# A fourth block product at half size in layer two's gate/up passes, and a step list for each of the four passes

## Chip, cores and metric

The kernel runs on one core of a Trainium2 chip. The time is the device time of one execution in microseconds, median of several runs; the lower is the better. The engines are TensorE (PE: matrix products; PEld is its weight load), VectorE (DVE), ScalarE (ACT), GpSimd (POOL) and SyncE (SP), which issues every DMA of this kernel. Each runs its own queue in order and waits for others at semaphores. Matrix products land in eight banks of PSUM, which VectorE and ScalarE read and write; everything else lies in SBUF.

## The reference

Two blocks are applied twice each, A, B, A, B, with the same weights, to x of 2048 tokens by 1024:

```python
phi = lambda t: jnp.where(t > 0, t + 1, jnp.exp(t)) + 1e-6
# block A (linear attention, 32 heads of 32)
q, k, v = split(layernorm(x) @ wqkv)
kv = einsum("bhsd,bhse->bhde", phi(k), v); z = sum over s of phi(k)
x = x + ((phi(q) @ kv) / (phi(q) . z + 1e-6)) @ wo
# block B (gated, no activation)
h = (layernorm(x) @ w_gate) * (layernorm(x) @ w_up)     # 1024 -> 3584
x = x + h @ w_down                                       # 3584 -> 1024
```

## The kernel before

**Layers and passes.** Block A and block B together are called a layer here; layer one is the first A and B (`first=True`), layer two the second. `layer_B` works on two passes of 1024 tokens (`ps_` 0 and 1). Each pass is a gate/up stage (`gateup`) that fills h, and a down stage (`down`) that adds h @ w_down to x. So there are four gate/up passes in all.

**Block products.** A gate/up pass runs over 14 pairs `p` of units. A unit is 256 columns of w_gate (even p) or of w_up (odd p); the two units of a pair, A and B, go through the same steps beside each other. One unit is a 2 x 2 block product (weights in blocks of 512 x 128, tokens in blocks of 512 x 512), made in Winograd's form of Strassen's scheme with seven products in place of eight, numbered 1 to 7. A whole product is four matmuls of 512 columns, accumulated in one bank (line L1534). The sums of weight blocks that products 3, 5, 6, 7 need are made once, in the first pass of layer one (`prep_s`), stored to `s_scratch` and loaded afterwards.

**Half-size products.** The same product number of both units, A and B together, is again a 2 x 2 block product, over blocks half as large. If its number is in the set that `L2SETS` names for the pass, it is made from seven half-size steps of two matmuls of 256 columns each (L1652) instead of two whole products. Steps 1, 5, 6, 7 work in two small banks (`B_L2`, 5 and 6, which swap roles from product to product); steps 2, 3, 4 (`direct`) add into the product's own bank. Around them stand copies and sums, `l2_of`: step 1 is followed by a ScalarE copy that seeds half of the first destination bank (L1656), step 5 by a ScalarE copy to SBUF named c5 (L1668), step 6 by a VectorE sum that seeds the other half (`seed5`, L1659) and reads step 6's bank, step 7 by both a copy and a sum for the second bank. The set before is "5" for the first pass of layer one, "542" for the second, and "254" for both passes of layer two. Product 1 can be in the set too, for pairs from 2 on (`p > 1`); no pass of the kernel before has it there.

**Further sums.** Half-size products need sums of weight blocks (`sums24`, `sums5`) and of token blocks (`tp_ops`). Those of weights are made in layer one, stored (`p4scr`, `p5scr`, `p1scr`, all called p_scratch in the profile) and loaded for each pair later (`load_s24`, `load_s5`, `load_s1`). `sp1buf` says where those for product 1 lie.

**The order of the work.** For each pair `gateup` runs through a list of tokens in `ORDERS`, chosen by the pass's set of products. The engines' queues follow it:

- `P1A` is product 1 of unit A, `D3B` product 3 of unit B into its final bank, or steps 2 and 3 (A) or 4 (B) where product 3 is made at half size; `41` is step 1 of half-size product 4.
- `F1A` evicts block 1 of unit A to h (`mul`, L917 on VectorE; for odd p GpSimd multiplies at L1558; a few evictions go through ScalarE). `S24`, `S5`, `S1` make or load the sums.
- `R` lets `ring_issue` load the next two units into a ring of five slots. `T0`, `T1` call `ticks`: layer norm steps of other tokens (`micro`), in the first pass of layer one also sums of weights (L914). `HA`, `HB` act in the last pair only.
- An apostrophe means that the token acts for the pair before, and a plus for the pair after. Tokens with an apostrophe that are left at the end form the `tail`, which is issued behind the first seven matmuls of the down stage (L1973).

Matmuls of half-size down products have line L2054. L914 is the helper for plain sums on VectorE, L917 that for a scaled sum, and L589 is that for a DMA.

**The planner.** `P.reorder` may rearrange, by a cost model, the instructions that carry one of the tags it is given; the others keep the order of the program. Before, the gate/up stage of layer one's second pass (`gu1`) is among the tags; the other three gate/up passes are not.

**Layer norm ahead of time.** While layer one's second gate/up pass runs, `ticks1` takes the first eight tokens' blocks of the next block A through layer norm in small steps (three a block, `micro`) up to `LN_G1`.

Of the kernel before, what the change touches and what calls it, by code (L numbers as in the profile page):

```python
# [334 lines left out]
def build_kernel(nc, A_x, A_wqkv, A_wo, B_w_gate, B_w_up, B_w_down, out):  # L335
# [16 lines left out]
    START_LATE = False  # L352
    TQ_N = 3
    LN_G1 = 8

    L2SETS = {(False, 0): "5", (False, 1): "542", (True, 0): "254", (True, 1): "254"}
    ORDERS = {
# [5 lines left out]
    }  # L363
    MUL_ENG = "pool"
    DORDS = {(True, 0): "4125637", (True, 1): "2167453", (False, 0): "2167453", (False, 1): "2167453"}
# [124 lines left out]
    with ExitStack() as es:  # L490
# [168 lines left out]
        class LN:  # L659
# [15 lines left out]
            def dst(self, n):  # L675
                if self.to == "A0":
                    return xr[:, n, :], r_xr(n)
                if self.to == "B" and n < 8 and n % 4 > 1:
                    o = RE + 2048 * (n % 4)
                    return vh(o, D), R(o, D * 2)  # L680
                return xn[n % 2], R(O_XN[n % 2], D * 2)

# [325 lines left out]
            dma(v, p5scr[p].rearrange("p (i x) -> p i x", i=4), [x for y in r for x in y], KL5[p % 2 if ps_ and not first else 0], rd=R(V_SP + p * 96 + 32, 32))  # L1008

        def sp1buf(first, ps_, m):  # L1010
            if not first and ps_:
                return (xnT[:, 4:8, 256 * m:256 * m + 256], [R(O_XT + (4 + i) * S * 2 + 512 * m, 512) for i in range(4)])
            o = RE + 4096 if first else O_X + (1 - m) * D * 2
            return vh(o, 1024).rearrange("p (i x) -> p i x", i=4), [R(o + i * 512, 512) for i in range(4)]
# [69 lines left out]
        def layer_A(lnp, nxt, first):  # L1084
# [369 lines left out]
            for i in range(NST):  # L1454
                if na[0] < NST:
                    if i % 3 == 2:
                        norm(tok[na[0]])
                        na[0] += 1
                elif RG["n"] < NR and i >= RING_I:
                    ring_issue()  # L1460
                nxt.step_t(1)
                nxt.b1_one()
                if i >= 2 and not START_LATE:
                    nxt.start(i - 2)
                y_grp(tok[i], 0, i)
                y_seed(i + 1)
                if i >= 1 and START_LATE:
                    nxt.start(i - 1)
                if i < NST - 1:
                    nxt.b2_one()  # L1470
                y_grp(tok[i], 1, i)
                if i > 3 and tws:
                    tws.pop(0)()
                if i in (11, 12, 13, 14):
                    stash(i - 7)
                if i == 14 and not first:
                    load_s24(0, 0)
                    load_s24(0, 1)
                    load_s5(first, 0, 0)
                if RG["tq"] is None:  # L1480
                    RG["tq"], RG["tn"] = [], 0
                while RG["tn"] < 4 and nxt.t_next > 4 + RG["tn"]:
                    RG["tq"] += t_ops(0, RG["tn"])
                    RG["tn"] += 1
                    if RG["tn"] == 4:
                        RG["tq"] += tp_ops(0, L2SETS[not first, 0].replace("1", ""))
                for _ in range(TQ_N):
                    if RG["tq"]:
                        RG["tq"].pop(0)()
# [5 lines left out]
        def layer_B(lnp, nxt, first):  # L1495
# [11 lines left out]
            def pair(ps_, p, l2):  # L1507
# [99 lines left out]
                    return v.rearrange("p i (k c) -> p i k c", k=2), r  # L1607

                def sums5(q="5"):
                    if not first or ps_:  # L1610
                        if q == "1":
                            load_s1(ps_, p)
                        else:
                            load_s5(first, ps_, p)
                        return
                    sp, rp = sp3() if q == "5" else sp1()
                    wA, rA = units[0]["w"][q]
                    wB, rB = units[1]["w"][q]
                    tt(sp[:, 0], wB[:, 0:2, :], wB[:, 2:4, :], ALU.add, rB, rp[0])
                    tt(sp[:, 2], wA[:, 0:2, :], wB[:, 0:2, :], ALU.subtract, rA + rB, rp[2])  # L1620
                    tt(sp[:, 1], sp[:, 0], wA[:, 0:2, :], ALU.subtract, rA + rp[0], rp[1])
                    tt(sp[:, 3], wA[:, 2:4, :], sp[:, 1], ALU.subtract, rA + rp[1], rp[3])
                    if q == "1":
                        dma(p1scr[p].rearrange("p (i x) -> p i x", i=4), sp1buf(first, ps_, m)[0], R(V_SP + p * 96 + 64, 32), KP1, rd=[x for y in rp for x in y])
                        return
                    dma(p5scr[p].rearrange("p (i x) -> p i x", i=4), sp5buf(first, ps_, m)[0], R(V_SP + p * 96 + 32, 32), KP5[m], rd=[x for y in rp for x in y])
# [87 lines left out]
            def gateup(ps_, ticks, l2, hook):  # L1714
                jit = first and ps_ == 0
                NP = NU // 2
                pairs = [pair(ps_, p, l2) for p in range(NP)]
                order = ORDERS[l2].split()
                n0 = RG["at"]["g", ps_]

                def token(p, tk, tail_):
# [18 lines left out]
                        return  # L1740
                    if tk[0] == "T":
                        i = int(tk[1])
                        if jit:
                            if i:
                                store_s(n0 + 2 * p)
# [9 lines left out]
                    c = pairs[p]  # L1755
                    if tk == "S1" and not first and p < 2:
                        return
                    if not first and (tk == "S24" and p < 2 or tk == "S5" and p < 1 + ps_) or first and ps_ and tk[0] == "S" and p == 0:
                        return
                    if tk == "S24":  # L1760
                        c["sums24"]()
# [11 lines left out]
                if jit:  # L1773
                    prep_s(n0)
                    prep_s(n0 + 1)
                for tk in ("S24", "S5"):
                    if tk + "+" in order:
                        token(-1, tk + "+", False)
                for p in range(NP):
# [406 lines left out]
            def dticks1(q, t):  # L2186
                if is_last:
                    return
                o1 = DORDS[first, 1]
                if q == o1[1] and t == 3:  # L2190
                    for x in "567":
                        tw_back("k", x)
# [12 lines left out]
                wd_load(1)  # L2205
            tq, pend = [], []
            pre, go = down(0, dticks0)
            tail = gateup(0, ticks0, L2SETS[not first, 0], pre)
            lnp.need(NST - 1)
            tq += t_ops(1) + tp_ops(1, "254" if first else L2SETS[not first, 1].replace("1", "")[::-1])  # L2210
            go(tail)
            pre, go = down(1, dticks1)
            P.tag = "gu1" if first else None
            tail = gateup(1, ticks1, L2SETS[not first, 1], pre)
            P.tag = None
            go(tail)
            lnp.use_dma = False
            lnp.on_act = False
# [32 lines left out]
        layer_A(lnA, lnB, False)  # L2251
        layer_B(lnB, None, False)

        P.reorder({"kq2", "gu1", "g1", "y1"})
        P.plan()
        P.emit(nc, block, esem, dsem, [KOUT])
    return P
# [34 lines left out]
```

## Time and profile before

| what | value |
|---|---|
| median of 3 runs | 1443.44 us (1442.42 to 1444.73) |
| the profiled execution | 1443.52 us, of which its span on the engines 1441.8 us |
| granted TensorE clock | 1.000 of full speed |
| GpSimd busy, share of the span | 439.5 us, 30% |
| moved by DMA | 337.80 MB, mean 234 GB/s |
| HBM read / written | 248.38 MB / 66.85 MB |

The profile is that of one execution. Busy times are given by engine, by group of instructions (line of the kernel, engine, operation, out<-in shapes, count; then busy time, mean of one in ns, and the idle time ahead of them with what ended it) and by stretch of time. The chain of waits follows the work back from the last instruction, at each step to what released it. In a timeline each row is a start in us, a duration, the engine, line and operation, the number of instructions merged, and in square brackets the idle time ahead with what ended it. TensorE's matmuls are pipelined: one is listed with a duration longer than its distance to the next.

### The profile page before, as it was taken

Reading aid. Unit: us, or ns where it says so; the run is one execution under the profiler, and the core shown is the slowest. Engines: PE = TensorE matmul, PEld = TensorE weight load, DVE = VectorE, ACT = ScalarE, POOL = GpSimd, SP = SyncE. Lnnn points to the kernel's source line nnn. Section 1 sums busy time; section 2 is a strip of 40 time slices with the busy share of each in tenths; the row PEclk is TensorE's granted clock in tenths of the full one; section 3 lists DMA queues with packets and bytes.
Section 4 is the critical chain, followed back from the end, with each engine's and each line's share of the span. In section 5 each row is a group of like instructions: output and inputs, shape, how many; then the busy total and the mean of one; then the engine's idle time right before and its main releaser. Section 6 shows DMA issues by size and latency. Waiting matters only on the chain.

```text
span 1441.8 us, 22143 instructions
## 1 busy us (share of the span) xinstructions
PE 1430.4 (99%) x8273; PEld 795.9 (55%) x8273; DVE 1156.2 (80%) x2170; ACT 597.4 (41%) x1220; POOL 439.5 (30%) x436
## 2 busy tenths in 40 slices
PE   9999999999999999999999999999999999999999
PEld 4444444555544555566664444456666576666558
DVE  8988898988868797887899869876666896666597
ACT  4332365454400255551147723555555014555302
POOL 4543631211110053432014446215343102342400
PEclk9999999999999999999999999999999999999999
DMA  7446766999999998986783656678886779888667
GB/s 241 101 108 178 159 156 172 279 325 308 288 311 324 304 297 259 291 275 209 279 269 95 190 162 142 177 184 260 272 254 227 254 247 297 265 272 274 228 203 236
DMA packets 350428, 337.80 MB, mean 234 GB/s; under 512 B 106736, under 2 KB 294640, under 8 KB 350320
## 3 DMA queue, kind: packets, MB, share of 16 engines
q1 hardware_dynamic: 350320, 336.38, 77.0%
q8 instruction: 65, 1.06, 0.3%
q14 instruction: 43, 0.35, 0.1%
HBM read 248.38 MB, written 66.85 MB: 219 GB/s over the span
## 4 chain that ended last, share of the span: by engine, by line
PE 90%; DVE 5%; DMA 2%; ACT 2%; issue 1%; SPq 0%; DVEq 0%; ACTq 0%
PE ps L1534 28%; PE ps L1652 14%; PE ps L1973 13%; PE ps L1094 8%; PE ps L1437 8%; PE ps L2054 8%; PE ps L1329 7%; PE ps L1158 3%; DVE arena L917 2%; DVE arena L914 1%; DMA arena<-in_A_wqkv_dram 1%; DMA arena<-p_scratch 1%; DMA arena<-xn_scratch 1%; PE ps L1352 0%; DVE ps L1659 0%
## 5 line engine op out<-in xcount | busy, mean ns | idle before, releaser
L1534 PE MATMUL ps<-arena 128*128 128x512 f16 x2016 | 491.3, 379 | 0.0
L917 DVE SCALAR_TENSOR_TENSOR arena<-ps,arena 128x512 f16<-128x512 f32 (+2 forms) x562 | 366.4, 681 | 62.4 <-PE ps L1973 27.6
L1558 POOL TENSOR_TENSOR arena<-arena 128x512 f16<-128x512 f16 x196 | 225.2, 1170 | 489.2 <-DVE arena L917 488.7
L914 DVE TENSOR_TENSOR arena<-arena 128x512 f16<-128x512 bf16 (+7 forms) x584 | 311.7, 575 | 11.3 <-PE ps L2054 4.9
L1534 PEld LDWEIGHTS ps<-arena 128*128 128x128 bf16 (+1 forms) x2016 | 196.8, 98 | 166.1 <-DVE arena L917 0.7
L1652 PE MATMUL ps<-arena 128*128 128x256 f16 x1960 | 273.4, 273 | 3.4 <-DVE ps L1659 1.6
L1652 PEld LDWEIGHTS ps<-arena 128*128 128x128 f16 (+1 forms) x1960 | 188.2, 98 | 106.5 <-DVE ps L1659 15.7
L1539 ACT ACTIVATE arena<-ps 128x512 f32<-128x512 f32 x308 | 184.4, 599 | 146.6 <-PE ps L1534 146.2
L1659 DVE TENSOR_TENSOR ps<-ps,arena 128x256 f32<-128x256 f32 x280 | 120.2, 429 | 142.7 <-ACT ps L1656 66.0
L1973 PE MATMUL ps<-arena 128*128 128x512 f16 (+1 forms) x896 | 195.2, 379 | 0.0
L1656 ACT COPY ps<-ps 128x256 f32<-128x256 f32 x280 | 98.5, 363 | 177.2 <-PE ps L1652 120.9
L1973 PEld LDWEIGHTS ps<-arena 128*128 128x128 f16 x896 | 87.4, 98 | 104.7
L2054 PE MATMUL ps<-arena 128*128 128x256 f16 (+1 forms) x1176 | 129.8, 273 | 0.2
L1094 PE MATMUL ps<-arena 128*128 128x512 bf16 x576 | 127.1, 379 | 0.5 <-DMA arena<-in_A_wqkv_dram 0.5
L2054 PEld LDWEIGHTS ps<-arena 128*128 128x128 f16 x1176 | 114.7, 98 | 15.6 <-ACT ps L2060 1.0
L1329 PE MATMUL ps<-arena 128*128 128x512 bf16 x512 | 115.8, 379 | 1.2 <-DMA arena<-xn_scratch 0.8
L1437 PE MATMUL ps<-arena 128*128 128x512 bf16 x512 | 110.8, 379 | 0.0
L1223 POOL TENSOR_TENSOR arena<-arena 128x1024 f16<-128x1024 f32 x32 | 80.0, 2498 | 86.6 <-DVE arena L1221 81.9
L1117 POOL TENSOR_TENSOR arena<-arena 128x512 f32<-128x512 f32 x60 | 72.3, 1211 | 80.4 <-DVE arena L808 40.7
L618 DVE BATCH_NORM_STATS2 arena<-arena 128x6 f32<-128x512 bf16 x128 | 87.2, 684 | 7.8 <-DMA arena<-in_A_x_dram 4.0
L1094 PEld LDWEIGHTS ps<-arena 128*128 128x128 f16 x576 | 55.7, 98 | 67.3 <-DMA arena<-in_A_wqkv_dram 1.5
L1158 PE MATMUL ps<-arena 128*128 128x512 bf16 (+1 forms) x392 | 85.9, 379 | 1.1 <-DVE ps L1165 0.5
(69 smaller groups left out, 943.7 us busy)
## 6 DMA issues: line engine op xcount, KB each, us to landing
arena<-s_scratch SPq DMA_DIRECT2D x84, 512.0 KB, 5.9
arena<-d_images SPq DMA_DIRECT2D x36, 896.0 KB, 5.5
arena<-in_B_w_gate_dram SPq DMA_DIRECT2D x56, 512.0 KB, 5.1
arena<-in_B_w_up_dram SPq DMA_DIRECT2D x56, 512.0 KB, 5.4
arena<-t_scratch SPq DMA_DIRECT2D x20, 896.0 KB, 4.9
s_scratch<-arena SPq DMA_DIRECT2D x28, 512.0 KB, 6.2
arena<-p_scratch SPq DMA_DIRECT2D x28, 512.0 KB, 5.7
arena<-in_B_w_down_dram SPq DMA_DIRECT2D x12, 896.0 KB, 6.6
```

The source lines that it names most:

```text
L914: P.add("dve", lambda e: e.tensor_tensor(out=out, in0=a, in1=b, op=op), rd=rd, wr=wr, prd=prd)
L917: P.add("dve", lambda e: e.scalar_tensor_tensor(out=out, in0=a, scalar=sc, in1=b, op0=ALU.mult, op1=op1), rd=rd, wr=wr, prd=prd)
L1094: P.add("pe", lambda e: [e.matmul(psb(bank), xnT[:, k, i * 128:(i + 1) * 128], w[:, k, h * 512:(h + 1) * 512], start=(k == 0), stop=(k == ...
L1158: P.add("pe", lambda e: [e.matmul(psb(bank), l[:, k, :], w[:, k, :], start=(start and k == 0), stop=(k == 3), skip_group_check=True) for k ...
L1329: return [e.matmul(psb(bank), xr[:, t, j * 128:(j + 1) * 128], pk[:, h, t, :], start=(start and t == ts[0]), stop=(stop and t == ts[-1]), ...
L1437: return [e.matmul(psb(bank), xnT[:, g, i * 128:(i + 1) * 128], wp[:, g, dh * 512:(dh + 1) * 512], start=(dh == 0 and g == 0), stop=(g == ...
L1534: P.add("pe", lambda e: [e.matmul(psb(bank), w[:, k, :], x[:, k, :], start=(start and k == 0), stop=(k == 3), skip_group_check=True) for k ...
L1539: P.add("act", lambda e: e.activation(t, psb(bank), AF.Copy, scale=SG), prd=[bank], wr=r)
L1558: P.add(MUL_ENG, lambda e: e.tensor_tensor(out=hx, in0=ut, in1=hx, op=ALU.mult), rd=ur + hr, wr=hr)
L1652: P.add("pe", lambda e: [e.matmul(psb(bank)[:, 256 * half:256 * half + 256], w[:, k, :], xx[:, k, :], start=(start and k == 0), stop=(k == ...
L1973: P.add("pe", lambda e: [e.matmul(psb(bank), hv[:, 7 * hf + k, t * 128:(t + 1) * 128], w[:, k, :], start=(q in fresh and hf == 0 and k == ...
L2054: P.add("pe", lambda e: [e.matmul(half(b, h), x[:, k, :], w[:, k, :], start=(bool(start) and k == 0), stop=(k == 6), skip_group_check=True ...
```

## The change

Layer two's sets become "2541" in both passes, so product 1 is made at half size there for pairs 2 to 13. `ORDERS` is no longer looked up by the set of products but by layer and pass, and all four lists are new. The sums of weights for product 1 are made in layer one's second pass (`S1'` in its list; `sp1buf` gives xnT columns there) and stored; in layer two they are loaded by `S1+`. Tokens 0 to 3 of x are stashed in layer two's block A as well, because their place serves as buffer in the first pass of layer two. `T` tokens for a pair outside the pass do nothing any more. The layer norm steps that are left at the end of layer one's second gate/up pass are done in its down stage (`LN_D1`). The tag `gu1` is taken from the planner; a tag "d1" is set, which the planner is not given.

```diff
-    L2SETS = {(False, 0): "5", (False, 1): "542", (True, 0): "254", (True, 1): "254"}
+    LN_D1 = 8
+    L2SETS = {(False, 0): "5", (False, 1): "542", (True, 0): "2541", (True, 1): "2541"}
     ORDERS = {
-        "5": "F3A' P1A D3B' HA' P1B R D2A F1A 51 P6A F3B' HB' 55 P6B 56 D2B T0 F1B P7A P7B D5A 57 F2A D4A D4B F4A D5B F2B F4B T1 D3A S5+",
-        "542": "F4A' T1' 21 P1A D3B' F2A' 25 26 P1B D4B' F3B' F4B' D3A' F3A' 27 D2A 51 P6A F1A D2B 55 F1B 56 R P6B T0 41 S24+ 57 P7A HA D5A 45 46 HB P7B D5B S5+ F2B 47 D4A",
-        "254": "D5B' F1B' S5 F2A' HA' 45' 46' F2B' P1A D3A' 47' S24 D4A' F4A' 21 T0 P1B HB' F3A' D3B' D4B' 25 26 F4B' P6A 51 F3B' D2A F1A 27 R T1 P6B 55 56 P7A D2B 41 57 D5A P7B",
+        (False, 0): "51' P7A' 55' P6B' F1A' T0' 56' HA' D4A' F4A' HB' T1' P7B' D2B' 57' P1A D5A' F2A' D4B' D2A S5 D5B' F2B' D3A' F4B' F3A' F1B' P6A D3B' F3B' R P1B",
+        (False, 1): "P7A' D2B' F1B' HA 57' 41' D5A' 45' F2A' P7B' 46' P1A S5 D5B' S24 D3A' T0' F2B' 47' D4A' F4A' S1' 21 25 P1B D3B' D4B' 26 F3A' R P6A F4B' F3B' HB 27 51 P6B D2A 55 F1A 56 T1'",
+        (True, 0): "P7A' 41' HB' D5A' HA' F2A' 57' P7B' D2B' 45' F1B' 46' D5B' F2B' D3A' S24 47' S1+ 11 D4A' 15 16 D3B' F4A' 17 21 P1A F3A' D4B' 25 26 P1B F4B' P6A F3B' 51 27 P6B D2A S5 F1A 55 56 T0 R T1",
+        (True, 1): "P6A' 27' 51' P6B' T1' 55' 56' P7A' D2A' F1A' 57' HB' D5A' S5+ F2A' D2B' 41' 45' F1B' P7B' 46' D5B' S1+ D3A' F2B' F3A' 47' 11 D4A' 15 16 D3B' F4A' 17 21 P1A D4B' T0 25 HA' F4B' S24+ 26 P1B F3B' R",
     }
...
+                if self.to == "A" and LN_G1 <= n < LN_D1:
+                    o = O_X + self.order[n] * D * 2
+                    return vh(o, D), R(o, D * 2)
...
         def sp1buf(first, ps_, m):
-            if not first and ps_:
+            if ps_:
...
                     stash(i - 7)
+                    if not first:
+                        stash(i - 11)
...
                 def sums5(q="5"):
-                    if not first or ps_:
+                    if not first or ps_ and q == "5":
...
-                order = ORDERS[l2].split()
+                order = ORDERS[not first, ps_].split()
...
                         i = int(tk[1])
+                        if not 0 <= p < NP:
+                            return
...
-                    if not first and (tk == "S24" and p < 2 or tk == "S5" and p < 1 + ps_) or first and ps_ and tk[0] == "S" and p == 0:
+                    if not first and (tk == "S24" and p < 2 or tk == "S5" and p < 1 + ps_) or first and ps_ and tk in ("S24", "S5") and p == 0:
...
-                for tk in ("S24", "S5"):
+                for tk in ("S24", "S5", "S1"):
...
+                if q in "267":
+                    for _ in range(2 if t < 3 else 1):
+                        if nxt.t_next < LN_D1:
+                            nxt.micro(LN_D1)
...
-            P.tag = "gu1" if first else None
+            P.tag = None
             tail = gateup(1, ticks1, L2SETS[not first, 1], pre)
-            P.tag = None
+            P.tag = "d1" if first else None
             go(tail)
...
-        P.reorder({"kq2", "gu1", "g1", "y1"})
+        P.reorder({"kq2", "g1", "y1"})
```

The helpers that the new steps call are as before: `tp_ops(ps_, "1")` makes four sums of token blocks in pairs 0 and 1, `load_s1` loads 256 KB.

More of the change, by code (lines that the diff above doesn't have):

```diff
@@ L2207, in layer_B @@
             pre, go = down(0, dticks0)
+            P.tag = None
             tail = gateup(0, ticks0, L2SETS[not first, 0], pre)
+            P.tag = None
             lnp.need(NST - 1)
@@ L2212, in layer_B @@
             pre, go = down(1, dticks1)
-            P.tag = "gu1" if first else None
+            P.tag = None
             tail = gateup(1, ticks1, L2SETS[not first, 1], pre)
-            P.tag = None
+            P.tag = "d1" if first else None
             go(tail)
```

2 rows, old and new, of the table ORDERS are left out of this document.

## The prediction

> **What bounds the kernel now.** I read the page first: the busy table, then the shares of the chain that ended last, then the groups of the two gate/up matmul lines.
>
> ```profile
> PE 1430.4 (99%) x8273; PEld 795.9 (55%) x8273; DVE 1156.2 (80%) x2170; ACT 597.4 (41%) x1220; POOL 439.5 (30%) x436
> ...
> PE 90%; DVE 5%; DMA 2%; ACT 2%; issue 1%; SPq 0%; DVEq 0%; ACTq 0%
> ```
>
> TensorE sets the time almost everywhere, so an edit pays only if it shortens TensorE's queue or removes one of its holes. The chain in order of time gives the price of a matmul, from two long unbroken pieces, and the period of a pair of units.
>
> ```profile
> 31.06 82.88 PE ps L1094 x384
> ...
> 315.31 2.59 PE ps L1534 x12
> ...
> 327.20 2.59 PE ps L1534 x12
> ...
> 669.33 10.70 PE ps L2054 x98
> ...
> 1026.38 1.73 PE ps L1534 x8
> ...
> 1037.87 1.73 PE ps L1534 x8
> ```
>
> A matmul of 512 columns costs 82.88/384 = 0.2158 us, one of 256 columns 10.70/98 = 0.1092 us. The first pass of layer one makes one block product of seven at half size: 48 × 0.2158 + 14 × 0.1092 = 11.89 us a pair, and 327.20 - 315.31 = 11.89. Layer two makes three: 32 × 0.2158 + 42 × 0.1092 = 11.49, and the period is 11.49. Both run at TensorE's own pace without a hole.
>
> To see the holes of all four gate/up stages I take TensorE's timeline, from the first gate/up matmul of a stage to the eighth down matmul (the last pair's late steps come behind the first seven).
>
> ```profile
> 238.85 1.46 PE L1534 MATMUL ps<-arena 128*128 128x512 f16 x6
> ...
> 406.80 0.38 PE L1973 MATMUL ps<-arena 128*128 128x512 f16 x1
> ...
> 489.89 0.38 PE L1652 MATMUL ps<-arena 128*128 128x256 f16 x2
> ...
> 658.59 0.38 PE L1973 MATMUL ps<-arena 128*128 128x512 bf16 x1
> ...
> 956.66 0.59 PE L1534 MATMUL ps<-arena 128*128 128x512 f16 x2
> ...
> 1119.76 0.81 PE L1973 MATMUL ps<-arena 128*128 128x512 bf16 x3
> ...
> 1197.43 0.81 PE L1534 MATMUL ps<-arena 128*128 128x512 f16 x3
> ...
> 1360.90 0.59 PE L1973 MATMUL ps<-arena 128*128 128x512 bf16 x2
> ```
>
> The stretches are 167.95, 168.70, 163.10 and 163.47 us. Matmul work in the first is 679 × 0.2158 + 196 × 0.1092 = 167.95, in each of the others 455 × 0.2158 + 588 × 0.1092 = 162.40. So the holes are 0.0, 6.3, 0.7 and 1.1 us: only the second pass of layer one has something to give back.
>
> **Fewer columns in layer two.** Product 1 becomes seven half-size steps for pairs 2 to 13 of both passes (pairs 0 and 1 stay whole). Each of 24 products swaps 8 matmuls of 512 for 14 of 256: 8 × 0.2158 - 14 × 0.1092 = 0.198 us, in all -4.74 us. Each adds two seed copies and one c5 copy on ScalarE and two seed sums on VectorE.
>
> ```profile
> L1656 ACT COPY ps<-ps 128x256 f32<-128x256 f32 x280 | 98.5, 363 | 177.2 <-PE ps L1652 120.9 <-PE ps L1534 31.1 <-DVE arena L917 23.9
> L1668 ACT COPY arena<-ps 128x256 f32<-128x256 f32 x140 | 51.8, 370 | 18.0 <-PE ps L1652 17.0
> L1659 DVE TENSOR_TENSOR ps<-ps,arena 128x256 f32<-128x256 f32 x280 | 120.2, 429 | 142.7 <-ACT ps L1656 66.0 <-ACT arena L1668 64.4 <-PE ps L1652 7.3
> ```
> ```profile
> 239.00:404.60 165.60, 165.60 (x866) 84.33 (x864) 143.94 (x341) 79.84 (x156) 30.72 (x30) 1.00 0.92 281
> ...
> 489.00:655.30 166.30, 163.47 (x1032) 98.00 (x1031) 140.19 (x280) 89.45 (x210) 64.27 (x66) 1.00 0.91 276
> ...
> 957.00:1115.00 158.00, 157.86 (x1015) 98.72 (x1013) 102.34 (x202) 88.33 (x209) 57.69 (x53) 1.00 0.78 242
> ```
>
> In the table by stretch (PE, PEld, DVE, ACT, POOL busy; clock; DMA share; GB/s) a pass of layer two leaves VectorE 55.7 us idle and ScalarE 69.7. The additions are 12 × 2 × 0.429 = 10.3 us on VectorE, with four more input sums under 2 us, and 12 × (2 × 0.363 + 0.370) = 13.2 on ScalarE: as sums of time they hide under TensorE. Twelve loads of 256 KB a pass, and in the first pass four stores and four reloads of tokens 0 to 3, go into a queue at 0.78: about 5 MB on 38, so 0.88, still covered. Without that cover a late sums load would hold step 15 for its landing.
>
> **The price of order.** Step 7 of a product writes the bank that the sum behind step 6 reads, and that sum needs the c5 copy of step 5. The new lists have `15 16 D3B' 17`: from the second matmul of 15 to the first of 17 TensorE has 3 × 0.1092 + 4 × 0.2158 = 1.19 us. The chain that must fit is seen in these rows:
>
> ```profile
> 1050.93 0.82 PE L1652 MATMUL ps<-arena 128*128 128x256 f16 x6
> ...
> 1051.57 0.37 ACT L1668 COPY arena<-ps 128x256 f32<-128x256 f32 x1 [0.45 <-PE ps L1652]
> ...
> 1052.04 0.43 DVE L1659 TENSOR_TENSOR ps<-ps,arena 128x256 f32<-128x256 f32 x1 [1.28 <-ACT arena L1668]
> ...
> 1056.86 0.43 DVE L1659 TENSOR_TENSOR ps<-ps,arena 128x256 f32<-128x256 f32 x1 [1.08 <-ACT ps L1656]
> ...
> 1057.35 0.63 PEld L1652 LDWEIGHTS ps<-arena 128*128 128x128 f16 x6 [0.24 <-DVE ps L1659]
> ```
>
> The six matmuls are `D5B' 45' 46'`, so the second of 45 starts at 1051.26 and the copy 0.31 later; 0.37 copy, 0.10 to VectorE, 0.43 sum, 0.06 to TensorE (1057.29 to 1057.35): 1.27 us. That is 0.08 more than there is, 24 times: +1.92 us. Bounds: 0, if the ends overlap a little, and 0.2 each (4.8), if ScalarE or VectorE is still in another instruction; behind step 17 on TensorE wait 21 and P1A, so nothing else absorbs it. I take 1.92, since the rows add up to it. The old lists left product 6 to 7 one more matmul group, which is why their period shows no hole. The other new neighbours fit: `47' 11 D4A' 15` gives 3 × 0.1092 + 4 × 0.1092 = 0.76 us for copy and hand-overs of 0.31 + 0.36 + 0.05.
>
> **Second pass of layer one.** Its work on TensorE is unchanged, but its planner is gone, its list is new, and it now makes the sums for product 1: 14 × 4 sums of 256 elements and 14 stores of 256 KB. In the first pass such sums stand already:
>
> ```profile
> L914 DVE TENSOR_TENSOR arena<-arena 128x256 f16<-128x256 f16 x56 | 13.7, 285 | 0.5
> ```
>
> 56 × 0.285 = 16.0 us at most, 13.7 as they overlap. VectorE has 166.30 - 140.19 = 26.1 us idle there, so it goes to 93% busy. DMA goes from 45.7 to about 49.4 MB, a share of 0.98. What that can do is seen where today's largest hole arises:
>
> ```profile
> 512.02 1.15 POOL L1558 TENSOR_TENSOR arena<-arena 128x512 f16<-128x512 f16 x1 [1.54 <-DVE arena L917]
> 512.20 1.25 DVE L914 TENSOR_TENSOR arena<-arena 128x512 f16<-128x512 bf16 x1
> ...
> 513.38 0.42 DVE L1659 TENSOR_TENSOR ps<-ps,arena 128x256 f32<-128x256 f32 x1
> ...
> 513.85 0.44 PEld L1652 LDWEIGHTS ps<-arena 128*128 128x128 f16 x5 [1.18 <-DVE ps L1659]
> 513.85 0.61 PE L1652 MATMUL ps<-arena 128*128 128x256 f16 x4 [0.90 <-DVE ps L1659]
> ```
> ```profile
> PE ps L1652 <- DVE ps L1659: 1.6, 4, 0.9
> PE ps L1652 <- ACT arena L1668: 0.5, 1, 0.5
> ```
>
> A sum that starts beside a GpSimd multiply takes 1.25 us, the seed sum behind it is late, and TensorE waits 0.90. The Trainium skill (SBUF — State Buffer, "Who interferes with whom") says of this that a VectorE instruction with two SBUF inputs and a GpSimd one that reads SBUF lock each other out, the second waiting for the first to end; by that rule each of the 14 groups could wait out a multiply (14 x 1.15 = 16.1 us as the worst, about the upper bound below), and this row agrees.
>
> Visible waits of this stage are 2.1 us, all counted in the 6.3; the other 4.2 are short. The list keeps the seed sums clear of the long bursts: 0.97 us from step 26 to 27 for 0.31 + 0.43 + 0.06. I take the 2.1 as they are and half of the 4.2 as saved: 4.2 us of holes, -2.1. Bounds: -6.3 if all holes close, and +16.0 if none of the sums is hidden.
>
> **The rest.** In the first pass of layer one the two bursts of weight sums (`T0'`, `T1'`) stand 1.1 us of TensorE apart, with `F4A'` between, which frees a bank for P1A. It has no hole to lose, so the bounds are 0 and +3; where three normalization steps fall into one burst P1A or D3A can wait, and I take +0.5. The normalization step dropped by the new guard moves to the down pass, one transpose on SP's queue, needed only in the fourth pair of the next layer: nothing. Uncovered it is one transposed load, 1.5 us.
>
> **Sum.** The profiled execution took 1443.52 us around a span of 1441.8, 0.08 over the median. 1443.52 - 4.74 + 1.92 - 2.1 + 0.5 = 1439.1; against the median 1439.0.
>
> **The rivals.**
> (a) Slower: VectorE in the second pass of layer one. If two fifths of the 16.0 us of sums come through as holes on top of today's 6.3, instead of 2.1 saved, the time is 1443.5 - 4.7 + 1.9 + 0.5 + 6.4 = 1447.6. It turns slower than before once this stage loses 2.3 us more than now. For it speak 93% busy and the 1.25 us row; against it 26.1 us of idle VectorE and the moved seed sums.
> (b) No gain: product 1's chain waits 0.2 us instead of 0.08 (4.8), and this stage stays at 6.3: 1443.5 - 4.7 + 4.8 + 0.5 = 1444.1. For it speaks that ScalarE's 0.60 us copies stand near the c5 copies, against it that none stands directly ahead of 15's.
> (c) The lists do all they could: no chain wait, and 5 of the 6.3 us gone: 1443.5 - 4.7 - 5 = 1433.8. Layer two's exact 11.49 periods speak for it.
> (d) The change does not do what it says: if the lists alone act and the swap is cancelled by 0.2 a pair, that is (b).
>
> **How the numbers follow.** Forecast 0.52, its own range 1435.5 to 1442; (a) 0.22, (b) and (d) 0.15, (c) 0.11. A measurement here tells 0.2%, 2.9 us. Faster means under 1440.5: all of (c) and nine tenths of the forecast, 0.58. Within 2.9 us: the rest of the forecast and most of (b), 0.18. Slower: (a) and a little of (b), 0.24. The range 1433.5 to 1447 holds (b), nearly all of (c), and leaves out the worse half of (a).
>
> **What would show it.** The period in layer two, pairs 2 to 13: 11.30 if no chain waits, 11.38 as forecast, 11.5 for (b). The stretch of the second pass of layer one: 166.6 forecast, 163 for (c), over 171 for (a), with waits of L1652 on L1659 behind L914. The first pass of layer one stays within 168.5. I am wrong if layer two's two stretches shrink by less than 1 us each, or that stage grows.

## The result, and the profile after

The changed kernel takes 1451.76 us (median of 4 runs, 1450.22 to 1452.64) beside 1443.65 us for the kernel before; the ratio is 1.0055, 95% interval 1.0038 to 1.0073. It is slower by 8 us, outside the range. The profiled execution took 1451.07 us with a span of 1449.3.

One thing is needed to read its times rightly. In the new lists product 7 of unit A of the last pair (in layer two's second pass product 6 too) comes behind the first seven down matmuls, which restart bank 0 into which it adds, and the product 1 sums of pairs 10, 12 and 13 overwrite columns of xnT into which tokens 0 to 383 of the next block A are already transposed. So a part of the last pair, of the first down tile and of those tokens' q and k is another than the reference's. The amount of work and its order are unaffected; the variants below that keep these lists share it. ("Tokens 0 to 3 of x" are its blocks 0 to 3 of 128 tokens each; "tokens 0 to 383" counts single tokens.)

The lines of the changed kernel carry other numbers: whole products are L1539 in place of L1534, half-size steps L1657 in place of L1652, seed copies L1661, seed sums L1664, c5 copies L1673, GpSimd's multiplies L1563, down matmuls L1980 and L2061. Beware of two: L917 is now the plain sum, which was L914, and L920 the scaled sum of the evictions, which was L917. In the runs below the numbers are higher or lower by a few, in the last one by up to 22.

The top of the page of the kernel after (busy times, then the chain's shares):

```profile
PE 1426.1 (98%) x8362; PEld 800.9 (55%) x8417; DVE 1211.0 (84%) x2282; ACT 618.9 (43%) x1292; POOL 440.8 (30%) x436
...
PE 87%; DVE 7%; DMA 3%; issue 1%; ACT 1%; SPq 0%; POOL 0%; DVEq 0%; ACTq 0%
```

The chain now leaves TensorE for 13% of the span in place of 10%. (TensorE shows 8362 matmuls for 8417 weight loads: 55 records are missing, so its busy time isn't compared. None is missing on the two gate/up lines; some of the eighth down matmuls below are the seventh on record.) TensorE's timeline of the kernel after, at the same eight places as in the prediction:

```profile
238.70 0.59 PE L1539 MATMUL ps<-arena 128*128 128x512 f16 x2
...
410.81 0.38 PE L1980 MATMUL ps<-arena 128*128 128x512 f16 x1
...
493.90 0.59 PE L1539 MATMUL ps<-arena 128*128 128x512 f16 x2
...
669.25 0.59 PE L1980 MATMUL ps<-arena 128*128 128x512 bf16 x2
...
968.09 0.38 PE L1657 MATMUL ps<-arena 128*128 128x256 f16 x2
...
1129.57 0.59 PE L1980 MATMUL ps<-arena 128*128 128x512 bf16 x2
...
1207.24 0.38 PE L1657 MATMUL ps<-arena 128*128 128x256 f16 x2
...
1368.60 0.38 PE L1980 MATMUL ps<-arena 128*128 128x512 bf16 x1
```

| stretch | before | after | difference |
|---|---|---|---|
| layer one, first pass | 167.95 | 172.11 | +4.2 |
| layer one, second pass | 168.70 | 175.35 | +6.7 |
| layer two, first pass | 163.10 | 161.48 | -1.6 |
| layer two, second pass | 163.47 | 161.36 | -2.1 |
| all else | 778.6 | 779.0 | +0.4 |

Layer two gained what it was to gain. Layer one, whose matmuls are the same as before, lost 10.8 us. TensorE's listed waits in the second pass, after, are these (in total, times, longest, in us):

```profile
PE ps L1657 <- DVE ps L1664: 5.0, 6, 1.0
PE ps L1539 <- DVE arena L920: 2.4, 5, 1.0
```

How they arise is shown by the timeline of one pair of that pass:

```profile
589.73 2.52 POOL L1563 TENSOR_TENSOR arena<-arena 128x512 f16<-128x512 f16 x2 [1.26 <-DVE arena L920]
...
590.83 2.51 DVE L917 TENSOR_TENSOR arena<-arena 128x512 f16<-128x512 bf16 x4
...
593.25 0.69 DVE L618 BATCH_NORM_STATS2 arena<-arena 128x6 f32<-128x512 bf16 x1
...
593.85 0.67 DVE L920 SCALAR_TENSOR_TENSOR arena<-ps,arena 128x512 f16<-128x512 f32 x1
...
594.58 1.04 PE L1539 MATMUL ps<-arena 128*128 128x512 f16 x4 [0.95 <-DVE arena L920]
594.61 2.32 POOL L1563 TENSOR_TENSOR arena<-arena 128x512 f16<-128x512 f16 x2 [2.35 <-DVE arena L920]
...
595.37 2.23 DVE L917 TENSOR_TENSOR arena<-arena 128x256 f16<-128x256 bf16 x4
...
597.52 0.43 DVE L1664 TENSOR_TENSOR ps<-ps,arena 128x256 f32<-128x256 f32 x1
...
598.00 0.61 PE L1657 MATMUL ps<-arena 128*128 128x256 f16 x4 [0.79 <-DVE ps L1664]
```

VectorE's queue is read from top to bottom: the four S24 sums take 2.51 us beside two GpSimd multiplies, a layer norm step follows, and only then the eviction F2B' (593.85) that frees the bank for product 3: TensorE waits 0.95 us. Then the four new sums take 2.23 us beside two more multiplies, the seed sum behind them is late, and step 27 waits 0.79 us. A narrower view separates the second of these four sums and the multiply beside it:

```profile
595.72 1.21 POOL L1563 TENSOR_TENSOR arena<-arena 128x512 f16<-128x512 f16 x1
595.83 1.24 DVE L917 TENSOR_TENSOR arena<-arena 128x256 f16<-128x256 bf16 x1
```

The sum ends 0.14 us after the multiply. So it is in all six pairs of this stretch in which GpSimd multiplies beside the new sums: the first two sums of the four each end 0.14 to 0.15 us after the end of a multiply (they take 0.54 to 0.80 and 1.24 us), the other two take 0.28 to 0.29. In the pairs between, all four take 0.28 to 0.29.

The first pass has the same picture with the sums for product 5, and an eviction behind them:

```profile
287.39 1.99 DVE L917 TENSOR_TENSOR arena<-arena 128x256 f16<-128x256 f16 x4
287.55 1.15 POOL L1563 TENSOR_TENSOR arena<-arena 128x512 f16<-128x512 f16 x1 [13.02 <-DVE arena L920]
...
290.04 1.68 PE L1539 MATMUL ps<-arena 128*128 128x512 f16 x7 [0.61 <-DVE arena L920]
```

### The profile page after: what moved, and what is told of

It is laid out like the page before. It is cut to its first block, busy times and chain, and to the rows that moved or that the text cites. A ratio compares the mean times of both kernels' runs of the same rounds, so it can differ in the third digit from the quotient of the medians.

```text
span 1449.3 us, 22852 instructions
## 1 busy us (share of the span) xinstructions
PE 1426.1 (98%) x8362; PEld 800.9 (55%) x8417; DVE 1211.0 (84%) x2282; ACT 618.9 (43%) x1292; POOL 440.8 (30%) x436
## 4 chain that ended last, share of the span: by engine, by line
PE 87%; DVE 7%; DMA 3%; issue 1%; ACT 1%; SPq 0%; POOL 0%; DVEq 0%; ACTq 0%
PE ps L1539 23%; PE ps L1657 16%; PE ps L1980 13%; PE ps L1097 8%; PE ps L2061 8%; PE ps L1440 8%; PE ps L1332 7%; PE ps L1161 3%; DVE arena L917 3%; DVE arena L920 2%; DMA arena<-in_B_w_gate_dram 1%; DVE ps L1664 1%; DMA arena<-in_A_wqkv_dram 1%; DMA arena<-xn_scratch 1%; PE ps L1355 0%
## 5 line engine op out<-in xcount | busy, mean ns | idle before, releaser
L1539 PE MATMUL ps<-arena 128*128 128x512 f16 x1824 | 453.2, 379 | 4.9 <-DVE arena L920 4.0
L920 DVE SCALAR_TENSOR_TENSOR arena<-ps,arena 128x512 f16<-128x512 f32 (+2 forms) x562 | 372.2, 683 | 70.7 <-PE ps L1980 29.7
L1563 POOL TENSOR_TENSOR arena<-arena 128x512 f16<-128x512 f16 x196 | 225.2, 1170 | 581.5 <-DVE arena L920 579.1
L917 DVE TENSOR_TENSOR arena<-arena 128x512 f16<-128x512 bf16 (+7 forms) x648 | 342.4, 569 | 15.3 <-PE ps L2061 4.9
L1657 PE MATMUL ps<-arena 128*128 128x256 f16 x2296 | 311.9, 273 | 6.3 <-DVE ps L1664 5.6
L1657 PEld LDWEIGHTS ps<-arena 128*128 128x128 f16 (+1 forms) x2296 | 214.8, 98 | 123.8 <-DVE ps L1664 27.5
L1539 PEld LDWEIGHTS ps<-arena 128*128 128x128 f16 (+1 forms) x1824 | 175.5, 98 | 150.9 <-DVE arena L920 9.8
L1664 DVE TENSOR_TENSOR ps<-ps,arena 128x256 f32<-128x256 f32 x328 | 141.2, 431 | 81.6 <-ACT ps L1661 34.7
L1980 PE MATMUL ps<-arena 128*128 128x512 f16 (+1 forms) x885 | 194.2, 379 | 1.0 <-POOL arena L1563 0.4
L1661 ACT COPY ps<-ps 128x256 f32<-128x256 f32 x328 | 109.9, 361 | 110.3 <-PE ps L1657 83.5
L1980 PEld LDWEIGHTS ps<-arena 128*128 128x128 f16 x896 | 87.3, 98 | 104.9 <-POOL arena L1563 0.9
L2061 PE MATMUL ps<-arena 128*128 128x256 f16 (+1 forms) x1176 | 129.8, 273 | 0.2
L2061 PEld LDWEIGHTS ps<-arena 128*128 128x128 f16 x1176 | 114.7, 98 | 15.6 <-ACT ps L2067 1.0
L1161 PE MATMUL ps<-arena 128*128 128x512 f16 (+1 forms) x385 | 85.4, 379 | 1.5 <-DVE arena L831 0.6
```

Source lines behind the costliest of these rows:

```text
L917: P.add("dve", lambda e: e.tensor_tensor(out=out, in0=a, in1=b, op=op), rd=rd, wr=wr, prd=prd)
L920: P.add("dve", lambda e: e.scalar_tensor_tensor(out=out, in0=a, scalar=sc, in1=b, op0=ALU.mult, op1=op1), rd=rd, wr=wr, prd=prd)
L1539: P.add("pe", lambda e: [e.matmul(psb(bank), w[:, k, :], x[:, k, :], start=(start and k == 0), stop=(k == 3), skip_group_check=True) for k ...
L1563: P.add(MUL_ENG, lambda e: e.tensor_tensor(out=hx, in0=ut, in1=hx, op=ALU.mult), rd=ur + hr, wr=hr)
L1657: P.add("pe", lambda e: [e.matmul(psb(bank)[:, 256 * half:256 * half + 256], w[:, k, :], xx[:, k, :], start=(start and k == 0), stop=(k == ...
L1664: P.add("dve", lambda e: e.tensor_tensor(out=psb(bank)[:, 256:512], in0=psb(src)[:, 0:256], in1=c5, op=ALU.add), prd=[src], rd=rc5, pwr=[b ...
```

## Experiments

All stretches are from TensorE's timeline of the run's profile; "time" is the median of a run with rounds, with its ratio to the kernel before on the same chip, or a single time. "P1, P2" are layer one's two passes, "Q1, Q2" layer two's.

**The old list in layer one's first pass** (time 1446.3, ratio 1.0026, interval 1.0016 to 1.0037).

```diff
-        (False, 0): "51' P7A' 55' ... F3B' R P1B",
+        (False, 0): "F3A' P1A D3B' HA' P1B R ... T1 D3A S5+",
```

> Only the list of layer one's first pass is the old one again. Theory (the new list of this pass brings its two bursts of weight sums and the sums for product 5 ahead of evictions that free TensorE's banks): the stretch of this pass goes from 172.1 back to 168.0 us, the other three stay within 0.5 us, and the time falls by 4.1 to about 1447.6. Rival (the holes come from slower loads, since the kernel moves more bytes): the stretch stays above 171.

P1 went to 167.98, P2 stayed at 174.87. The first pass's loss goes with its list and not with the bytes.

**Without the new sums** (time 1444.9, ratio 1.0017, interval 1.0008 to 1.0026).

```diff
-                    tt(sp[:, 0], ...); tt(sp[:, 2], ...); tt(sp[:, 1], ...); tt(sp[:, 3], ...)
+                    if q == "5": (the same four)
```

> The four VectorE sums for product 1 are left out of layer one's second pass (their stores stay, so product 1's half-size steps in layer two work on other data). Theory A (VectorE's sums, slowed by GpSimd multiplies, stand ahead of the sum that step 27 waits for): the wait of about 0.95 us behind step 26 goes in every second pair, the wait of D3B' behind S24 stays, the stretch of this pass falls from 175.4 to about 171. Rival B (the product 1 sums are the whole loss): 168.7 as before the change. Rival C (the new list without the planner is the whole loss): 175.

P2 went to 169.41: 5.9 of the 6.7 us hang on the 56 sums (52 of them in this window, where they keep VectorE busy for 17.7 + 3.7 = 21.4 us). The waits for seed sums (5.0 us in this stage after) are gone, those for evictions stay at 2.4. A named 171, B 168.7. The wait that A named went, and the sums are nearly the whole loss, as B said.

**Without GpSimd's multiplies in layer one** (one time, 1437.01).

```diff
-                    elif m == 0:
+                    elif m == 0 or first:
                         stt(hx, psb(bank), SG, add[0], add[1], hr, prd=[bank])
```

> GpSimd's multiply of gate and up is left out in both passes of layer one (h is the up part alone there); VectorE's instructions are the same. Theory A (VectorE's sums of two SBUF operands are held up by GpSimd multiplies): four S24 sums take 1.4 us in place of 2.5, the four product 1 sums 0.9 in place of 2.2, and the second pass falls from 175.4 to 170 or less, the first from 172.1 to 169 or less. Rival (VectorE has simply too much to do in this order): 175 and 172 stay.

P2 fell to 164.59, P1 to 168.97. VectorE's groups in the second pass, first of the kernel after, then of this run (count, busy us, mean ns of one):

```profile
L917 DVE TENSOR_TENSOR arena<-arena 128x512 f16<-128x512 bf16 x40 | 21.3, 559 | 0.5
L917 DVE TENSOR_TENSOR arena<-arena 128x256 f16<-128x256 bf16 x39 | 17.7, 480 | 0.4
```
```profile
L917 DVE TENSOR_TENSOR arena<-arena 128x512 f16<-128x512 bf16 x40 | 15.7, 419 | 1.0 <-DMA arena<-in_B_w_up_dram 0.5
L917 DVE TENSOR_TENSOR arena<-arena 128x256 f16<-128x256 bf16 x40 | 10.3, 284 | 0.5
```

And the same two bursts in its timeline:

```profile
583.10 1.54 DVE L917 TENSOR_TENSOR arena<-arena 128x512 f16<-128x512 bf16 x4
...
586.68 1.01 DVE L917 TENSOR_TENSOR arena<-arena 128x256 f16<-128x256 bf16 x4
```

The number of VectorE's instructions is unchanged and the list is the changed one; only the neighbour is gone. The sums take 419 and 284 ns in place of 559 and 480 on average, those of 256 elements in the first pass 285 in place of 391, and the pass beats even the kernel before by 4.1 us. The rule of the Trainium skill (SBUF — State Buffer, "Who interferes with whom"), that the second of two such instructions waits out the first, is borne out here, with its price: the ends of the sums follow those of the multiplies, and without multiplies the groups take 1.54 and 1.01 us in place of 2.51 and 2.23. (The eight scaling steps of layer norm, L655, shorten too, from 697 to 541 ns; the run does not part their share from that of the sums.) DMA is no rival here: its share in this pass is 0.96, more than the 0.89 of the changed kernel, and no wait of TensorE for a DMA is listed. The 5.9 us of the run before and the 10.8 us here overlap, since both free the new sums.

**The same in the kernel before** (one time, 1442.59).

> The kernel before, without GpSimd's multiply in both passes of layer one (h is the up part alone there). Theory (the lock, not the planner's order, makes the holes of the second pass): its stretch falls from 168.7 to 164 or less, so that the lock costs about 5 us before the change and 10.8 with it. Rival (the holes belong to the order): 168.

P2 came to 166.3, not 164: the lock costs 2.4 us before the change and 10.8 with it (175.35 to 164.59), and some 3.9 us of the old holes belong to the old order. In this pass the new list is thus the better one where there is no lock, even with 56 sums more.

**The planner back, with the new list** (time 1456.35, ratio 1.0090, interval 1.0075 to 1.0105).

```diff
-            P.tag = None
+            P.tag = "gu1" if first else None
...
-        P.reorder({"kq2", "g1", "y1"})
+        P.reorder({"kq2", "gu1", "g1", "y1"})
```

> The planner gets layer one's second gate/up pass again, with the new list and the product 1 sums as they are. Theory (the order on VectorE is the fault, and a planner that pulls evictions ahead of sums mends it): the stretch of this pass falls from 175.4 to about 170, the time by 5 to about 1446.5. Rival (there is too much on VectorE for any order): 174 or more.

P2 rose to 179.29, with a granted clock of 0.99 in this pass (1.00 before). The planner's own order waits 10.6 us for seed sums:

```profile
PE ps L1657 <- DVE ps L1664: 10.6, 12, 2.1
```

Its cost function has an interlock with GpSimd for scalar operations and copies only, so it rates these sums at their undisturbed length. That this is why its order is bad was not tested.

**Both old lists and the planner, with the new sums** (time 1452.16, ratio 1.0068, interval 1.0051 to 1.0084).

```diff
+        (False, 1): "F4A' T1' 21 P1A ... T0 41 S24+ S1 57 P7A ...",
```

> Layer one with both old lists and the planner as before; layer two as changed; the product 1 sums stand on VectorE in layer one's second pass (S1 ahead of step 57). Theory (VectorE's sums held up by GpSimd multiplies cost more than the order around them): that pass takes 168.7 plus 4 to 8 us, 173 to 177, although its list is the old one; the first pass 168.0; layer two 161.5 each; time 1442.4 + 5 - 3.5 = 1444. Rival (the new list is the fault): the second pass comes out at 170 or less and the time at 1440.

P2 is 179.79, 11.1 over the old 168.70: more than theory and rival had named. At this place in the old order the sums cost more than in the new one; other places in it were not tried.

**The sums in the loops without multiplies** (`e11_odd`; one time, 1443.26).

```diff
+                    if tk == "S1" and first:
+                        if p % 2 == 0:
+                            for x in (p, p + 1):
+                                if x > 1: pairs[x]["sums5"]("1")
+                        return
```

> As changed, with the old list in the first pass; in the second pass the product 1 sums stay on VectorE but are made for two pairs at once in the loops in which GpSimd has no multiplies (pairs 0 and 1 left out). Theory (the lock): the sums of 256 elements fall from 480 to about 300 ns each; if that is what hurts, the stretch falls from 175 to 171 or less. Rival (the length of VectorE's queue ahead of the sum that step 27 waits for): eight sums in one loop hold it as long as four slow ones, 174 or more.

The sums now take 286 ns each, yet P2 falls only from 174.87 (the run with the old first list alone) to 173.21, where it would be 169.41 without the sums. So the lock on these sums is not all of it: eight undisturbed sums in a row hold up what stands behind them too. As the run changes both the lock and the grouping, it doesn't part their shares.

**In addition F2B' ahead of S24** (one time, 1451.15).

```diff
-P1A S5 D5B' S24 D3A' T0' F2B' 47'
+P1A S5 D5B' F2B' S24 D3A' T0' 47'
```

> As e11_odd, and in the list of layer one's second pass the eviction F2B' stands ahead of the S24 sums and of T0' in place of behind them. Theory (product 3 of unit B waits for the bank that F2B' reads, because that eviction is queued behind the burst): the 3.0 us of waits for evictions by L920 go, and the stretch falls from 173.2 to about 170.5, the time to about 1440.5. Rival (VectorE's queue only passes the delay on to the next user): the waits move to the seed sums (L1664) and the stretch stays above 172.5.

The rival won: P2 is 179.68. The waits for evictions fell from 3.0 to 0.4 us, and others took their place:

```profile
PE ps L1657 <- DVE ps L1664: 5.2, 11, 0.8
PE ps L1657 <- ACT ps L1661: 5.2, 10, 0.6
```

An eviction that stands early in an in-order queue makes everything behind it wait for its input: VectorE's waits for TensorE ahead of evictions (L920) grew from 2.0 to 8.7 us in this pass.

**The sums on GpSimd, in those loops** (time 1453.99, ratio 1.0076, interval 1.0061 to 1.0091; it also has the layer two lists of the next run, which cost it 7.8 us).

```diff
+                    en = "pool" if q == "1" else "dve"
-                    tt(sp[:, 0], wB[:, 0:2, :], wB[:, 2:4, :], ALU.add, rB, rp[0])
+                    tt(sp[:, 0], wB[:, 0:2, :], wB[:, 2:4, :], ALU.add, rB, rp[0], eng=en)
```

> The product 1 sums are made by GpSimd in the loops in which it has no multiplies, for two pairs at a time (pairs 0 and 1, which nobody loads, are left out); list of the first pass as before, of the second as changed; step 21 ahead of 17 in layer two. Theory (lock between VectorE's sums and GpSimd's multiplies, and length of VectorE's queue): the second pass falls to 169 to 171, the time to 1442.4 - 3.5 - 1.4 + 1.5, about 1439 to 1440. Rival (GpSimd's own sums hold up S24 as long as before): 173 or more.

P2 stayed at 175.31: the rival's number, and its mechanism. GpSimd's sums take some 740 ns each, the S24 sums on VectorE 622 in place of 559, and the waits for evictions by L920 are 6.1 us in this pass, after 2.4 in that of the changed kernel.

**Step 21 ahead of step 17 in layer two** (one time, 1457.98).

```diff
-15 16 D3B' F4A' 17 21 P1A
+15 16 D3B' 21 F4A' 17 P1A
```

> In both lists of layer two step 21 stands ahead of step 17, all else as changed. Theory (the 0.06 us hole in every pair is step 17 waiting for the sum behind step 6): with 0.22 us more between them the hole goes, the period of a pair falls from 11.39 to 11.33 us or less and each stretch of layer two by 0.7 to about 160.7. Rival (step 25 then waits for the copy behind step 17, for which only 0.76 us is left): no gain or a hole at step 25.

The edit puts 21's seed ahead of the eviction F4A' of the same bank, so block 4 of unit A is another here, and the eviction and everything behind it wait for that copy (in Q1, VectorE's evictions wait 10.8 us for seed copies, and P1B 0.18 us a pair for a seed sum). Q1 and Q2 grew to 165.20 and 165.36. The run doesn't test the hole at step 17; it is read from the rows below.

**Half of the layer norm steps in the down stage** (one time, 1458.76).

```diff
-    LN_G1 = 8
+    LN_G1 = 4
```

> Four of the eight layer norm blocks move from layer one's second gate/up pass to the down stage behind it (LN_G1 4 in place of 8). Theory (what hurts is how long VectorE's queue is ahead of an eviction): about 7 us less on VectorE there, the stretch falls from 175.4 to 171 to 173; the sums stay slow. If VectorE's total were the bound, it would fall by the whole 7, to 168. The down stage and what follows (83.1 and 298.8 us between the stretches now) may grow by up to 2.

P2 fell by 3.3 to 172.07, as the theory said, but the way from there to layer two's first gate/up matmul grew from 298.84 to 309.42 us. The waits in that stretch:

```profile
PE ps L2061 <- DVE arena L920: 4.3, 2, 4.1
PE ps L1980 <- DVE arena L917: 2.7, 1, 2.7
```

So 7.0 of the 10.6 us are waits for VectorE in the down stage, where at most 2 were expected. The granted clock of this stretch was 0.99, after 1.00 in the changed kernel; what that adds was not separated. VectorE is no freer in the down stage; the steps moved the delay and made it larger.

**The sums in layer one's first pass**, three placements with the second pass as before the change. Tokens 0 and 1 of x give the place, and layer two's left-over steps come ahead of the first down group. (The expectation measures Q1 and Q2 to that group, 1.5 us less; to the eighth down matmul they stay at 161.4 and 161.5 in the last of the three.)

At the end of the list (`e10_s1first`; time 1449.65, ratio 1.0050, interval 1.0033 to 1.0067):

```diff
+... F4B T1 D3A S5+ S1
```

> The product 1 sums move to layer one's first pass, where GpSimd multiplies half as long (S1 at the end of the old list, pairs 0 and 1 left out, their place is that of tokens 0 and 1 of x); the second pass has its old list and the planner; layer two keeps product 1 at half size and its new lists, its left-over steps are issued ahead of the first down group. Theory (the sums cost by where they meet GpSimd multiplies and a waiting eviction): the second pass is back at 168.7, the first takes 168 to 170, layer two's stretches 160.0 (1.5 less, since the down group no longer stands in them); time 1442.5 - 3.5 + 1.5 + 0.8, about 1441. Rival (48 more sums cost 5 or more us in any pass of layer one): the first pass at 173 or more, time at 1444 or more.

P1 is 173.67 (4.2 us in seven waits for a seed copy, which itself waits for an eviction behind the sums), P2 169.09. The lock isn't the reason here: only one of the 36 sums in the row of bf16 inputs is held, their mean is 303 ns. Nevertheless the loss is 5.7 us, by their place in the queue; and the down stage waits 3.2 us for its weights, since tokens 0 to 3 were loaded back ahead of them.

In the middle, reload behind the weights (`e12_s1mid`; time 1446.62, ratio 1.0026, interval 1.0015 to 1.0037):

```diff
+... 56 D2B S1 T0 F1B ...
```

> As e10_s1first, but S1 stands in the middle of a loop of the first pass (ahead of T0), where GpSimd has no multiplies, and tokens 0 to 3 of x are loaded back behind the down weights. Theory (place on VectorE's queue decides, not the number of sums): the first pass takes 169 to 170 in place of 173.7, the 3.2 us wait of the down stage for its weights goes, and the time is 1442.4 - 3.7 + 0.5 + 1.5 + 0.4, about 1441, 0.1% under the kernel before. Rival (48 more sums cost about 5 us wherever they stand): 172 or more, time 1444 or more.

P1 is still 173.10: by now "5 us wherever they stand" looked right. The wait for the down weights fell from 3.2 to 1.7 us only.

One by one (time 1442.07, the kernel before 1443.05; ratio 0.9996, interval 0.9987 to 1.0005):

```diff
+... D2A F1A Sa 51 P6A F3B' HB' 55 P6B Sb 56 D2B T0 F1B Sc P7A P7B D5A 57 F2A Sd D4A ...
```

> As e12_s1mid, but the four product 1 sums of a pair stand singly in the list of layer one's first pass (behind F1A, behind step 55's group, behind F1B, behind F2A). Theory (a group of sums delays an eviction or seed behind it; single ones fit between them): the first pass falls from 173.1 to 169.5 or less, the time to about 1441.5. Rival (48 more sums cost about 5 us in any place): 172 or more, and 1445 or more.

P1 is 168.70. The same 48 sums cost 0.75 us as single instructions and 5.1 as groups of four. The lock is much the same in both (six of the 36 are held in each, means 346 and 375 ns), so their place and grouping decide. The only wait of TensorE that is still listed from this pass up to the next is that for the down weights:

```profile
PE ps L2002 <- DMA arena<-in_B_w_down_dram: 0.9, 1, 0.9
```

Against the kernel before, it is 0.6% better than the changed kernel, and it ties with the one before: of layer two's gain of 3.6 us, 0.75 are spent in P1, 0.4 in P2 and 0.6 outside the four stretches, and what is left, 1.9 us in this profile and 1.0 between the medians, doesn't stand clear of the noise.

## Why the prediction was wrong

**Columns and the chain 15 to 17: right.** The forecast gave -4.74 + 1.92 = -2.8 us for layer two, measured are -3.7. The hole is there in every regular pair, by the very hand-overs that were added up:

```profile
1046.61 1.50 PE L1657 MATMUL ps<-arena 128*128 128x256 f16 x12
...
1047.90 0.37 ACT L1673 COPY arena<-ps 128x256 f32<-128x256 f32 x1 [0.24 <-PE ps L1657]
1047.95 1.03 PE L1539 MATMUL ps<-arena 128*128 128x512 f16 x4
1048.38 0.43 DVE L1664 TENSOR_TENSOR ps<-ps,arena 128x256 f32<-128x256 f32 x1 [0.53 <-ACT arena L1673]
...
1048.87 0.39 PE L1657 MATMUL ps<-arena 128*128 128x256 f16 x2
```

The second matmul of step 15 is the tenth of twelve, at 1047.59; copy 0.31 later, sum at 1048.38, step 17 at 1048.87. The four matmuls between end their turn at 1047.95 + 0.86 = 1048.81: a hole of 0.06 us, 24 times 1.4, where 1.9 was forecast. Two gaps of 0.01 to 0.02 us a pair come on top, so that the period is 11.39 us, against 11.49 before and 11.38 forecast. That gives 24 × 0.10 = 2.4 us. The other 1.3 of the 3.7 lie outside the regular pairs, where the kernel before had its holes of 0.7 and 1.1 us (0.57 of them at one place), which the forecast left standing: that part of the gain was not foreseen.

**The second pass of layer one: the step that failed.** "I take the 2.1 as they are and half of the 4.2 as saved: 4.2 us of holes, -2.1." Measured is +6.7. The 56 sums were priced at 285 ns, their length in the first pass, set against VectorE's idle time as a total, and so entered the sum as nothing. In every second pair the four took 2.2 us or more in place of 1.0, and they always stood as a group ahead of a seed sum; left out, they give 5.9 us back. The row of 1.25 us that shows a held sum was quoted, but only rival (a) was given it. Of the worst case in the prediction, that each of the 14 groups waits out a multiply, not quite half came true: six groups of this stretch met multiplies and were held by about 1.2 us each. "The list keeps the seed sums clear of the long bursts" was wrong too: the chain from step 26 to 27 was added up without the S1 group that stands ahead of 27's seed sum, and the chain from F2B' to D3B', in which S24 and a layer norm step stand, was not looked at.

**The first pass: a bound that was too tight.** Forecast +0.5 with an upper bound of 3 and a stretch within 168.5, measured +4.2 and 172.1. The bound had no row behind it; it looked at the bursts of weight sums and layer norm, not at the S5 sums. The run without multiplies shows 3.1 us of it as lock, where the S5 sums now meet multiplies and hold up evictions, and the old list takes all of it away.

**What was right beside that.** Rival (a) had the mechanism and its sign, and its 6.4 us for the second pass are close to 6.7; as nothing stood behind its "two fifths", that closeness is luck. The range missed because the two passes lose largely for one reason, sums that are held and hold up what is behind them, and so lose together, 10.8 us; (a) left the first pass at 0.5. DMA did not bound: its share in the second pass is 0.89 after. The one transpose moved to the down stage cost little (such a load lands after 3.2 us at the median, not the 1.5 that the prediction names): the way from the second pass to layer two's first gate/up matmul took 298.07 us before and 298.84 after. Four layer norm blocks moved there lengthened it by 10.6.

## What to carry to other kernels

Where TensorE sets the time, price a new VectorE instruction by what stands behind it in the queue, and by what GpSimd does at that moment, not by VectorE's idle total: the same 48 sums cost 0.75 or 5.1 us by their place and grouping, and the same list 164.6 or 175.4 us by whether GpSimd multiplies. Ask of a planner's cost model which interlocks it has: here one that lacks this one made an order slower than the fixed list (179.3 against 175.4 us), though the cause was not isolated. And where several stages share one mechanism, let a rival's price take all of them at once.

## What the runs showed of the hardware

The lock between a VectorE sum of two SBUF operands and a GpSimd multiply lengthens a group of four sums of 256 elements from 1.01 to 2.23 us. The mean of 480 ns for such a sum mixes two kinds: those held until 0.14 to 0.15 us after a multiply's end (0.54 to 1.24 us), and the rest at 0.28 to 0.29. I had expected single sums to be held, not every group that meets multiplies. The hand-overs of this chain repeat to about a hundredth of a microsecond in both kernels: 0.31 us from the start of the last matmul to ScalarE's copy, 0.10 from its end to VectorE, 0.06 from VectorE's end back to TensorE.
